# Retention and two FFNs: the loads of q and k parted by tokens from the fourth chunk on

## The chip, the cores and the metric

The program runs on one core of a Trainium2 chip. The metric is the device time of one execution in microseconds (us), as the median of several runs. TensorE is called PE here, VectorE DVE, ScalarE ACT, GpSimd POOL and SyncE SP; PE's loads of its weights are PEld.

## What is computed

A retention layer over two batches, eight heads, 768 tokens and 64 channels, in float32, then two feed-forward layers (FFNs) on its output, 1536 tokens by 512. The layers are cut here to what matters:

```python
for b in range(nb):                                   # blocks of tokens
    intra = einsum('bhic,bhjc->bhij', qb, kb) * Dmask # Dmask: powers of lam
    intra = einsum('bhij,bhjd->bhid', intra, vb)
    inter = einsum('bhid,bhde->bhie', qb * lam_pow, kv_state)
    out[:, :, sl] = intra + inter
    kv_state = lam_block * kv_state + einsum('bhsd,bhse->bhde', kb * rev_pow, vb)
x = out as (1536, 512)
x = mish(x @ moe_w_in) @ moe_w_out                    # 512 -> 2048 -> 512
x = elu(x @ moe2_w_in) @ moe2_w_out
```

## The kernel before

**Retention** (lines 126 to 385) works on twelve chunks of 128 tokens, all eight heads of one batch at a time; chunk n is batch n % 2, tokens 128 * (n // 2) onwards. For each chunk q, k and v are loaded from HBM to tiles `qn`, `kn` and `vn` of 128 partitions (one token each) by 8 heads by 64 channels (`load`, lines 143 to 156). One transfer moves 256 KB; a piece of contiguous memory in it is one token of one head, 64 float32 or 256 bytes. Only chunk 0 is loaded in halves, of four heads each, so that work can begin early.

The loop at line 357 runs over n. At its head SP issues the loads of k and q of chunk n + 3 and of v of chunk n + 1, and in some rounds a weight tile of the first FFN (`raw`, 512 KB, `LOAD` at line 536). Then PE does, in this order: the scores of chunk n (`sc`, line 275), the transposes of chunk n + 1 (`Tp`, line 231, first k's, then q's, each in two halves of 64 tokens), and the outputs of chunk n - 1 (`o`, line 305: first the terms of q and the state `sbd`, then those of `am` and `vn`) with its new state (`st`, line 314). ACT copies the transposed tiles out of PSUM, DVE multiplies by the decay and keeps the state, POOL scales k (`kd`, line 255).

Four buffers stand behind each of `qn`, `kn` and `vn`, so a load waits only for the readers of the chunk four before. The order on each engine is that of the program (`pin`). All loads are issued by SP, one after the other, so an issue that is held holds all behind it. SP has eight semaphores for the completion of its DMAs and takes them in turn (DMAHW0 to DMAHW7 in the rows of the order below): a DMA waits until the one eight before it has landed.

**The FFNs** (lines 388 to 571) work on 512 tokens by 512 columns, with every float32 operand as a high and a low part and three matmuls for each product (lines 412 and 454). DVE and ACT make the two parts of each weight tile from `raw` (`w_steps`, lines 86 to 120); a few of these steps stand already in the last rounds of retention (`STEPS`, line 537), and SP loads each next weight tile when a buffer comes free (line 115).

Of the kernel before, what the change touches and what calls it, by code (L numbers as in the profile page):

```python
# [18 lines left out]
def kernel(  # L19
# [12 lines left out]
    nc = tc.nc  # L32
    P = 128
# [92 lines left out]
    def retention(beside_load, beside_step, at_end):  # L126
# [12 lines left out]
        def pin(ins):  # L139
            tc.keep_in_program_order(ins)  # L140
            return ins

        def load(n, names, parts=1):
            if not 0 <= n < NC:
                return
            b, c = chunks[n]
            for nm in names:
                nat[n, nm] = io.tile([P, H, D], F32, tag=nm + "n", name=nm + "n")
            for y in range(parts):
                for nm in names:  # L150
                    src, t = {"k": k, "q": q, "v": v}[nm], nat[n, nm]
                    hs = slice(y * H // parts, (y + 1) * H // parts)
                    pin(nc.sync.dma_start(  # L153
                        out=t[:, hs],
                        in_=src[b, hs, c * P:(c + 1) * P, :].rearrange("h p d -> p h d"),
                    ))

        lam_b = cst.tile([P, H, 1], F32, name="lam_b")
        load(0, "kq", 2)
        nc.scalar.dma_start(out=lam_b.rearrange("p h o -> p (h o)"), in_=lam.partition_broadcast(P))  # L160
        load(1, "kq")
        load(2, "kq")
        load(0, "v")

# [7 lines left out]
        def powers(m, end):  # L172
# [19 lines left out]
            out=eye, in_=eye, compare_op=ALU.not_equal, fill=1.0, base=0,  # L192
# [7 lines left out]
            out=dm.rearrange("p h i -> p (h i)"),  # L200
# [357 lines left out]
    def first_units():  # L558
        for _ in todo:
            pass  # L560
        for u in range(EARLY):
            unit(u)
            weights_at(u)

    retention(beside_load, beside_step, first_units)
    open_late()
    for u in range(EARLY):
# [36 lines left out]
```

## Time and profile before

| | us |
|---|---|
| median of 3 runs (lowest to highest) | 583.84 (583.68 to 584.41) |
| the profiled execution, device time | 584.55 |
| its span, first to last instruction | 582.4 |
| PE busy in the span | 575.6 (99%) |
| retention, up to the first FFN matmul | about 54 |

The profile is of one execution, whose device time is 2.15 us above its span and 0.71 us above the median. It shows PE in the granted clock of 2.4 GHz (1.00 of full speed) in all slices. The views used are the page, the instructions of PE and SP in order of time with what ended the idle time before them, the DMA queues of a stretch, the DMA issues of a stretch with their time to landing, and the busy time of a stretch. A queue named "instruction" carries the engines' own instructions; q1 carries SP's loads.

### The profile page before, as it was taken

To read this page: it belongs to the slowest core of one execution; us is meant where nothing else is said; L and a number is where in the kernel's file an instruction comes from. 1 tells how busy PE (TensorE), PEld (TensorE's weight loads), DVE (VectorE), ACT (ScalarE), POOL (GpSimd) and SP (SyncE) were. 2 spreads that over 40 slices of the span, in tenths; PEclk is the share of its full clock that TensorE was granted. 3 is DMA by queue.
4 is the path that set the end of the run, shared out by engine and by line. 5 is a ranking of instruction groups with operands and counts; after the bars stand their busy time and mean duration, and the time that the engine had idled before them with its cause. 6 is when DMAs were issued, how large, how long until landed. Compare 5 with 4: busy or idle time off the path is not lost.

```text
span 582.4 us, 8137 instructions
## 1 busy us (share of the span) xinstructions
PE 575.6 (99%) x3240; PEld 481.9 (83%) x3240; DVE 431.1 (74%) x798; ACT 231.5 (40%) x390; POOL 18.8 (3%) x28
## 2 busy tenths in 40 slices
PE   8999999999999999999999999999999999999997
PEld 7888888888888888888888888888888888888886
DVE  5779999998399726993599956995499957944342
ACT  3655554344134124233346445555145235235220
POOL 5330000000000000000000000000000000000000
PEclk9999999999999999999999999999999999999999
DMA  9998333344023301322022221321022310000112
GB/s 189 194 221 233 109 109 109 109 114 140 1 73 109 108 2 36 108 77 70 0 73 72 74 72 37 109 77 69 2 72 73 108 37 0 2 0 1 72 55 91
DMA packets 61029, 46.66 MB, mean 80 GB/s; under 512 B 38848, under 2 KB 55488, under 8 KB 60992
## 3 DMA queue, kind: packets, MB, share of 16 engines
q1 hardware_dynamic: 60848, 46.14, 27.8%
q8 instruction: 25, 0.41, 0.3%
q14 instruction: 12, 0.10, 0.1%
q10 hardware_dynamic: 144, 0.00, 0.0%
HBM read 43.00 MB, written 3.15 MB: 79 GB/s over the span
## 4 chain that ended last, share of the span: by engine, by line
PE 93%; DMA 2%; DVE 2%; SPq 2%; issue 0%; ACT 0%; ACTq 0%
PE h L412 44%; PE y L454 43%; DMA vn<-in_v_dram 2%; PE o L305 2%; PE y L469 2%; SPq L153 2%; PE sc L275 1%; PE st L314 0%; PE Tp L231 0%; DVE b L104 0%; DVE u L111 0%; DVE xl L333 0%; DVE q L263 0%; DVE am L283 0%; ACT T L237 0%
## 5 line engine op out<-in xcount | busy, mean ns | idle before, releaser
L412 PE MATMUL h<-xh,w 128*128 128x512 f32 x768 | 240.8, 389 | 0.2 <-ACT w L118 0.2
L412 PEld LDWEIGHTS h<-xh,w 128*128 128x128 f32 x768 | 144.2, 188 | 30.5 <-ACT w L118 0.6
L412 PE MATMUL h<-xl,w 128*128 128x512 f32 x384 | 149.4, 389 | 0.0
L454 PE MATMUL y<-w,g 128*128 128x512 f32 (+1 forms) x588 | 132.5, 385 | 0.0
L454 PEld LDWEIGHTS y<-w,g 128*128 128x128 f32 x588 | 108.9, 188 | 22.0
L454 PE MATMUL y<-g,w 128*128 128x512 f32 x528 | 121.5, 389 | 0.0
L454 PEld LDWEIGHTS y<-g,w 128*128 128x128 f32 x528 | 99.1, 188 | 20.5
L482 DVE TENSOR_TENSOR acc<-acc,y 128x512 f32<-128x512 f32 (+1 forms) x73 | 49.5, 679 | 58.5 <-PE y L454 58.5
L422 DVE TENSOR_TENSOR g<-g,g 128x512 fp32r<-128x512 f32 x96 | 66.0, 689 | 30.0 <-ACT g L421 27.2
L412 PEld LDWEIGHTS h<-xl,w 128*128 128x128 f32 x384 | 72.1, 188 | 14.8
L118 ACT ACTIVATE w<-m 128x512 fp32r<-128x512 f32 x64 | 40.2, 628 | 102.1 <-PE h L412 55.2
L421 ACT ACTIVATE g<-g 128x512 fp32r<-128x512 f32 x96 | 60.2, 628 | 16.3 <-DVE g L439 14.8
L119 DVE TENSOR_TENSOR w<-m,w 128x512 fp32r<-128x512 f32 x64 | 44.1, 688 | 24.3 <-ACT w L118 23.7
L430 ACT ACTIVATE g<-h 128x512 f32<-128x512 f32 x48 | 28.5, 597 | 71.1 <-PE h L412 71.1
L436 ACT ACTIVATE e<-h 128x512 f32<-128x512 f32 x48 | 28.6, 596 | 59.0 <-PE h L412 58.0
L439 DVE SCALAR_TENSOR_TENSOR g<-e,h 128x512 f32<-128x512 f32 x48 | 32.9, 685 | 17.0 <-ACT e L437 17.0
L104 DVE SCALAR_TENSOR_TENSOR b<-raw,b 128x512 int32<-128x512 int32 x64 | 44.3, 693 | 0.4
L111 DVE SCALAR_TENSOR_TENSOR u<-raw,u 128x512 f32<-128x512 uint32 x64 | 43.9, 687 | 0.2
L116 DVE TENSOR_TENSOR m<-b,u 128x512 f32<-128x512 f32 x64 | 43.9, 687 | 0.1
L437 ACT ACTIVATE e<-e 128x512 f32<-128x512 f32 x48 | 30.2, 630 | 1.1
L98 DVE TENSOR_SCALAR m<-m 128x512 f32<-128x512 f32 x64 | 27.3, 428 | 0.1
L107 DVE TENSOR_SCALAR u<-b 128x512 int32<-128x512 int32 x64 | 27.0, 423 | 0.4
(50 smaller groups left out, 306.2 us busy)
## 6 DMA issues: line engine op xcount, KB each, us to landing
raw<-in_moe_w_in_dram SPq DMA_DIRECT2D x32, 512.0 KB, 3.8
raw<-in_moe_w_out_dram SPq DMA_DIRECT2D x32, 512.0 KB, 3.3
vn<-in_v_dram SPq DMA_DIRECT2D x12, 256.0 KB, 5.5
kn<-in_k_dram SPq DMA_DIRECT2D x11, 256.0 KB, 5.2
qn<-in_q_dram SPq DMA_DIRECT2D x11, 256.0 KB, 5.2
out_dram<-acc SPq DMA_DIRECT2D x11, 256.0 KB, 2.0
kn<-in_k_dram SPq DMA_DIRECT2D x2, 128.0 KB, 3.1
qn<-in_q_dram SPq DMA_DIRECT2D x2, 128.0 KB, 3.3
```

What stands on the lines that cost most here:

```text
L104: yield nc.vector.scalar_tensor_tensor(out=b, in0=hw, scalar=-0x40000000, in1=b, op0=ALU.bitwise_and, op1=ALU.bitwise_or)
L111: yield nc.vector.scalar_tensor_tensor(out=uf, in0=lw, scalar=2.0 ** -52, in1=uf, op0=ALU.mult, op1=ALU.mult)
L116: yield nc.vector.tensor_tensor(out=mf, in0=bf, in1=uf, op=ALU.add)
L118: nc.scalar.activation(out=w[:, 0], in_=mf, func=AF.Copy)
L119: yield nc.vector.tensor_tensor(out=w[:, 1], in0=mf, in1=w[:, 0].bitcast(F32), op=ALU.subtract)
L412: nc.tensor.matmul(h, lhsT=lt, rhs=rt, start=(kk == 0 and n == 0), stop=(kk == KD - 1 and n == 2),)
L421: nc.scalar.activation(out=gg[:, 0], in_=g, func=AF.Copy)
L422: nc.vector.tensor_tensor(out=gg[:, 1], in0=g, in1=gg[:, 0].bitcast(F32), op=ALU.subtract)
L437: nc.scalar.activation(out=e, in_=e, func=AF.Exp, scale=-1.0)
L439: nc.vector.scalar_tensor_tensor(out=g, in0=e, scalar=-1.0, in1=h, op0=ALU.add, op1=ALU.max)
L454: nc.tensor.matmul(y, lhsT=lt, rhs=rt, start=(i == 0 and n == 0), stop=(i == G - 1 and n == 2),)
L482: nc.vector.tensor_tensor(out=dst, in0=dst, in1=y, op=ALU.add)
```

## The change

From chunk 3 on, `load` issues q in two DMAs instead of one, of tokens 0 to 119 and 120 to 127, and k in two: by n % 4 they are 126 and 2, 108 and 20, 117 and 11, 110 and 18 tokens. The transfer of v, the first three chunks and all else stay. The bytes and the pieces of 256 bytes are the same, 1024 to a tile.

```diff
+        def rows_of(n, nm):
+
+            if n < 3 or nm == "v":
+                return ()
+            if nm == "q":
+                return (120,)
+            return ((126,), (108,), (117,), (110,))[n % 4]
...
-                    pin(nc.sync.dma_start(
-                        out=t[:, hs],
-                        in_=src[b, hs, c * P:(c + 1) * P, :].rearrange("h p d -> p h d"),
-                    ))
+                    ends = (0,) + rows_of(n, nm) + (P,)
+                    for r0, r1 in zip(ends, ends[1:]):
+                        pin(nc.sync.dma_start(
+                            out=t[r0:r1, hs],
+                            in_=src[b, hs, c * P + r0:c * P + r1, :].rearrange("h p d -> p h d"),
+                        ))
```

Lines after it move down by ten. On SP, v of chunk 0, then k and q of chunk 3 and v of chunk 1 stand like this before:

```order
L153 DMA vn<-in_v_dram 128x8x64 [waits DMAHW1_49]
L153 DMA kn<-in_k_dram 128x8x64 [waits DMAHW2_49]
L153 DMA qn<-in_q_dram 128x8x64 [waits DMAHW3_49]
L153 DMA vn<-in_v_dram 128x8x64 [waits DMAHW4_49]
```

And now, with SP's row of a round three DMAs long before and five long after:

```order
L163 DMA vn<-in_v_dram 128x8x64 [waits DMAHW1_49]
L163 DMA kn<-in_k_dram 110x8x64 [waits DMAHW2_49]
L163 DMA kn<-in_k_dram 18x8x64 [waits DMAHW3_49]
L163 DMA qn<-in_q_dram 120x8x64 [waits DMAHW4_49]
L163 DMA qn<-in_q_dram 8x8x64 [waits DMAHW5_49]
L163 DMA vn<-in_v_dram 128x8x64 [waits DMAHW6_49]
```

Each chunk from the fourth on has two more DMAs, 18 in all, and two more of the eight completion semaphores. On PE the transposes of chunk 3 and the outputs of chunk 1 stand like this before:

```order
L231 MATMUL Tp<-ident,kn 128x64 [waits DMAHW2_49,DVE_49]
L231 MATMUL Tp<-ident,kn 128x64 x7
L231 MATMUL Tp<-ident,qn 128x64 [waits DMAHW3_49]
L231 MATMUL Tp<-ident,qn 128x64 x7
L305 MATMUL o<-am,vn 64x128 [waits DMAHW4_49,DVE_49]
L305 MATMUL o<-am,vn 64x128 x7
```

And now:

```order
L241 MATMUL Tp<-ident,kn 128x64 [waits DMAHW2_49,DVE_49]
L241 MATMUL Tp<-ident,kn 128x64 [waits DMAHW3_49]
L241 MATMUL Tp<-ident,kn 128x64 x6
L241 MATMUL Tp<-ident,qn 128x64 [waits DMAHW4_49]
L241 MATMUL Tp<-ident,qn 128x64 [waits DMAHW5_49]
L241 MATMUL Tp<-ident,qn 128x64 x6
L315 MATMUL o<-am,vn 64x128 [waits DMAHW6_49,DVE_49]
L315 MATMUL o<-am,vn 64x128 x7
```

The second matmul of each group, which reads the upper 64 tokens, waits for the second DMA. No instruction of PE, DVE, ACT or POOL is added or moved; POOL's `kd` waits for both DMAs of its k.

## Rows read from the trace of the kernel before

**Rows 1.** The page: busy us (share of the span) and instructions of each engine

```profile
PE 575.6 (99%) x3240; PEld 481.9 (83%) x3240; DVE 431.1 (74%) x798; ACT 231.5 (40%) x390; POOL 18.8 (3%) x28
```

**Rows 2.** TensorE in order of time: start us, us, line, out<-in, idle before

```profile
14.51 0.47 PE L231 MATMUL Tp<-ident,kn 64*128 64x64 f32 x8
...
16.36 1.09 PE L305 MATMUL o<-am,vn 128*64 128x128 f32 x16 [0.56 <-DMA vn<-in_v_dram]
...
22.79 0.41 PE L231 MATMUL Tp<-ident,kn 64*128 64x64 f32 x8
...
23.38 1.09 PE L305 MATMUL o<-q,sbd 128*64 128x128 f32 x16
```

**Rows 3.** TensorE in order of time, later in the same loop

```profile
33.64 1.16 PE L275 MATMUL sc<-T 64*128 64x128 f32 x16
...
36.16 1.04 PE L305 MATMUL o<-am,vn 128*64 128x128 f32 x16
...
37.59 1.16 PE L275 MATMUL sc<-T 64*128 64x128 f32 x16
...
41.34 1.09 PE L305 MATMUL o<-am,vn 128*64 128x128 f32 x16
```

**Rows 4.** SyncE in order of time: start us, us that the issue held it

```profile
2.85 0.51 SPq L153 DMA_DIRECT2D kn<-in_k_dram  x1
...
6.54 1.10 SPq L153 DMA_DIRECT2D vn<-in_v_dram  x1
7.68 1.32 SPq L153 DMA_DIRECT2D kn<-in_k_dram  x1
9.04 1.14 SPq L153 DMA_DIRECT2D qn<-in_q_dram  x1
10.23 1.14 SPq L153 DMA_DIRECT2D vn<-in_v_dram  x1
...
12.66 2.30 SPq L153 DMA_DIRECT2D qn<-in_q_dram  x1
...
25.78 2.17 SPq L153 DMA_DIRECT2D vn<-in_v_dram  x1
...
30.36 0.91 SPq L153 DMA_DIRECT2D vn<-in_v_dram  x1
31.32 1.53 SPq L75 DMA_DIRECT2D raw<-in_moe_w_in_dram  x1
...
34.67 2.45 SPq L153 DMA_DIRECT2D vn<-in_v_dram  x1
```

**Rows 5.** DMA queues of 12.0:14.5: packets, MB, share of 16 engines

```profile
q8 instruction: 1, 0.02, 3.3%
```

**Rows 6.** DMA of 14.5:19.2 in 40 slices of 0.12 us

```profile
GB/s 233 231 172 163 133 113 100 41 37 46 115 174 133 129 235 270 283 270 235 218 185 129 61 78 148 176 218 279 283 281 268 255 264 231 238 248 264 231 248 251
```

**Rows 7.** DMA issues at 6.54, 7.68, 9.04, 10.23: count, KB, us to landing

```profile
vn<-in_v_dram SPq DMA_DIRECT2D x1, 256.0 KB, 5.2
kn<-in_k_dram SPq DMA_DIRECT2D x1, 256.0 KB, 5.2
qn<-in_q_dram SPq DMA_DIRECT2D x1, 256.0 KB, 6.2
vn<-in_v_dram SPq DMA_DIRECT2D x1, 256.0 KB, 6.0
```

**Rows 8.** The same for the issues at 30.36, 31.32, 34.67

```profile
vn<-in_v_dram SPq DMA_DIRECT2D x1, 256.0 KB, 4.9
raw<-in_moe_w_in_dram SPq DMA_DIRECT2D x1, 512.0 KB, 6.1
vn<-in_v_dram SPq DMA_DIRECT2D x1, 256.0 KB, 6.6
```

**Rows 9.** Line 81 on SyncE, later: issue ns min/median/max

```profile
L81 SPq DMA_DIRECT2D raw<-in_moe_w_out_dram x32: 327/336/341, 51.5 to 467.2; - x32
```

**Rows 10.** 54 to 62 us: busy us (instructions) by engine, clock, DMA share, GB/s

```profile
54.00:62.00 8.00, 7.84 (x59) 6.29 (x58) 7.87 (x18) 2.62 (x5) 0.00 (x0) 1.00 0.28 90
```

## The prediction

> **What bounds the kernel now.** I read the page first: PE is busy for 575.6 of the 582.4 us [rows 1]. Most of that lies in the FFNs, behind the change, and there PE runs without a gap. So a gain can only be idle time of PE in retention, and it is kept only if what follows moves up with it. I then read PE in order of time and looked for the places where one round of the loop takes longer than the next. There are two where a DMA ended the wait.
>
> The first is in the round of chunk 2. From the first transpose of k to the outputs behind the transposes it takes 16.36 - 14.51 = 1.85 us; an undisturbed round takes 23.38 - 22.79 = 0.59 us. PE loses **1.26 us**, first to q of chunk 3, then to v of chunk 1 [rows 2]. The second is in the round of chunk 8. From the scores to the outputs on `vn` an undisturbed round takes 36.16 - 33.64 = 2.52 us, this one 41.34 - 37.59 = 3.75. PE loses **1.23 us** [rows 3]. Together that is 2.49 us, and it is all that the loads cost PE in the rounds that the change reaches.
>
> Next I asked why those loads are late. The landings stand in the rows of the single issues: v of chunk 0 at 6.54 + 5.2 = 11.7, k of chunk 3 at 7.68 + 5.2 = 12.9, q of chunk 3 at 9.04 + 6.2 = 15.2, v of chunk 1 at 10.23 + 6.0 = 16.2 [rows 4, 7]. One step is 1.2 us, the next 2.4, the next 1.0. The step of 2.4 us goes with one 16 KB packet of the instruction queue, the only one in 12.0 to 14.5 [rows 5]. It took 3.3% of 16 engines in 2.5 us, so 1.3 us of one engine. SP's issue of that time is held for 2.30 us, against 1.1 to 1.3 before it [rows 4], and then the whole stream falls to 37 GB/s for a moment, from above 230 [rows 6]. I read this as one DMA engine being blocked by the instruction fetch, its queue filling, SP standing at that queue, and the other fifteen running dry. Another issue that is held for over 2 us stands at 25.78 [rows 4].
>
> The second stall has the same cause summed up. From 11.7 to v of chunk 7 at 34.67 + 6.6 = 41.3 there are 21 transfers of 256 KB and one weight tile. The tile takes 37.4 - 35.3 = 2.1 us (31.32 + 6.1 against 30.36 + 4.9) [rows 4, 8], so the 21 take 27.5 us, 1.31 each. A round has three, 3.93 us, which is what PE needs for a round (37.59 - 33.64 = 3.95 [rows 3]). The stream has nothing to spare, and the weight tile puts it behind.
>
> **What the change does, part by part.**
>
> *The bytes* are the same and cost nothing.
>
> *Fewer tokens for some engines.* A DMA of fewer than 128 tokens need not use all sixteen engines evenly. If the engine that fetches instructions is among those relieved, it takes the 1.3 us of a fetch without holding SP, and a transfer returns to its step of 1.2 us (11.7 to 12.9 [rows 4, 7]). No row here tells how the tokens are dealt out, nor which engine fetches. The Trainium skill does ("DMA: Bandwidth & Descriptors", the section on why a DMA increments its semaphore by 16): a DMA from SP uses the largest number of engines up to 16 that divides its tokens, and the lowest-numbered ones. By that q would leave the last engine idle and k the last two to five, while the busiest engine carries 27 to 29 tokens of a chunk's three tensors instead of 24; at the two rates of the next paragraph the sum for a chunk would be 3.4 to 4.3 us by it. No run here shows that yet.
>
> *More tokens for others.* What is taken from some engines goes to the rest. At a step of 1.2 us for 8 tokens an engine takes 0.15 us per token. An engine that is behind does better: the step after the fetch is 1.0 us [rows 4, 7], 0.125 us per token. So the parting has a price between nothing (the full engines run at the rate of one that catches up) and 0.15 us for each small part (they run at the common rate, and one has a token more).
>
> *Eighteen more DMAs on SP.* The shortest issue in the trace takes 0.34 us (median of 32 [rows 9]), and the same 256 KB whose issue now takes 1.1 us took 0.51 when nothing stood before it [rows 4]. So SP is held by full queues, not by its own work: three issues at 0.51 and two at 0.34 are 2.2 us of a round of 3.95. Each is also issued over four transfers ahead (5.2 us to landing against 1.2 a step). The cost per small part lies between 0 and 0.34 us, and I take **0.07 us** for both prices together, a fifth of that end, since the queue ahead covers most of it and the engine's faster rate most of the rest.
>
> *More waits.* PE waits twice more in a chunk, before the second matmul of each group; behind it stand the transposes, the outputs and the next scores. The second part is issued right behind the first, so this is the old wait with a later name, and its cost is in the 0.07. POOL's `kd` waits for two DMAs; PE needs it only a round later. SP waits for the DMA eight before, now 1.6 chunks back (6.3 us at 3.95) instead of 2.7; landings take 4.9 to 6.6 us [rows 7, 8]. It may hold SP now and then, but seven DMAs, over four of them large, still stand in the queues, so I count nothing. If that cover is gone, it is the issue's 0.34 again.
>
> *The sum.* First stall: k, q and v after 11.7 land in three steps of 1.2, plus two small parts, 0.14: v of chunk 1 at 15.4. PE would reach it at 16.36 - 1.26 = 15.1, so with the 0.15 us that it started after the landing before, a stall of 0.45 remains and 0.8 us is gained (0 to 1.26). Second stall: 21 steps of 1.2, the tile's 2.1 and 14 small parts (seven chunks) of 0.07, 1.0: 25.2 + 2.1 + 1.0 = 28.3, so v of chunk 7 lands at 40.0 instead of 41.3. The first gain is part of this one. PE is **1.3 us** ahead at this point, and after it only two parted chunks follow. Ends: with the small parts at 0, v lands at 39.0, and PE is ahead by 2.3; with both stalls gone it is 2.49, the most that can be had. With 0.34 each, 14 cost 4.8, v lands at 43.8, and PE is 2.5 us behind.
>
> *Does the rest move up?* From 54 to 62 us DVE is busy for 7.87 of 8.00 and PE for 7.84 [rows 10]; DVE's chain there hangs on PE's last rounds, so both shift together. The weight tiles are in the same stream and move up too. I count no loss. The profiled execution would go from 584.55 to 583.2, the median from 583.84 to **582.5 us**.
>
> **The rivals.**
>
> *No difference: the price eats the relief.* With 0.15 us a small part, 14 cost 2.1, v of chunk 7 lands at 41.1, and 0.2 us is left: 583.6. For it speaks the step of 1.2 us that holds whenever all engines work; against it the 1.0 us after the fetch.
>
> *Slower: the fetching engine is not relieved.* If that engine is one of those that get more, each fetch still holds SP, and its own queue is longer. Then nothing of 2.49 is gained and the price comes on top: 18 parts of 0.15, 2.7 us, less what a round can hide. I take 2.4: 586.2. It decides as soon as the engine has a token more than before, and the rows say nothing against it but that the change takes its tokens always from the same end.
>
> *Slower: SP becomes the bound.* If each added issue costs its 0.34 us in the stream, PE is 2.5 us behind at v of chunk 7, and the last four parts add 1.4, of which a round can hide some 0.7: 3.2 us, 587.0. This begins where five issues no longer fit between two rounds; 2.2 of 3.95 us speak against it. A rule of the Trainium skill speaks for it: the same page ("Rules for kernel authors") says that transfers under 64 KB are mostly overhead and that a transfer parted by partitions gains nothing, because the parts share the engines. The small parts here are 4 to 40 KB; no row shows one of that size. By that rule the time is this rival's.
>
> *The relief is there and goes lost later*, in the DVE-bound stretch: the time would be that of no difference, and it is counted there.
>
> **How the numbers follow.** A measurement of this kernel can tell about 0.2%, 1.17 us, from no change. The forecast, faster by over 0.2%, has 0.47: 582.5, its own range 581.3 to 582.6. No difference has 0.28; its values reach from 582.7 to 585.0. An unrelieved engine has 0.18 and SP as the bound 0.07, both slower by over 0.2%. The range from 581.3 (both stalls gone) to 586.2 (the engine not relieved, taken whole) leaves out the SP rival and some of the tails, under 2 in 10. Faster 0.47, same 0.28, slower 0.25.
>
> **What would show it.** Right: no SP issue of over 2 us beside a packet of the instruction queue in the rounds of chunks 2 to 6; no dip of the stream near 15.4 us; q of chunk 3 landing before 14.8 and v of chunk 1 near 15.4; v of chunk 7 near 40; the first FFN matmul 1 to 2 us earlier, and the same number of us off the end. Wrong: steps of 1.3 us or more between landings of whole chunks' tensors without a fetch beside them, issues of the small parts near 0.5 us with nothing before them, or PE waiting for the second part of a k or q. If the landings move up and the end doesn't, the last step, that the rest follows, is what failed.

## The result, and the profile after

The change makes the kernel slower: 588.77 us (588.18 to 589.47, 4 runs) against 583.86 us (583.68 to 584.41), a ratio of 1.0074 with an interval of 1.0059 to 1.0089. That is 4.9 us where 1.3 us less were forecast. The profiled execution after took 588.18 us with a span of 586.0, against 584.55 and 582.4 before.

The page after: the busy time of PE, the packets of SP's queue, and the chain that ended last.

```profile
PE 578.6 (99%) x3240; PEld 484.2 (83%) x3240; DVE 430.7 (73%) x798; ACT 231.4 (39%) x390; POOL 19.1 (3%) x28
...
q1 hardware_dynamic: 60951, 46.15, 28.4%
...
PE h L422 44%; PE y L464 43%; DMA qn<-in_q_dram 4%; PE y L479 2%; SPq L163 2%; PE warm L225 1%; PE o L315 1%; PE sc L285 1%; PE Tp L241 1%; ACT T L247 0%; DVE u L111 0%; POOL kd L265 0%; DVE b L104 0%; DVE u L107 0%; PE st L324 0%
```

PE has the same 3240 matmuls as in [rows 1]. New in the chain is `qn<-in_q_dram`. The four longest pieces of that chain up to 60 us (start us, us, what) show where these loads sit.

```profile
23.81 4.59 DMA qn<-in_q_dram
...
31.43 5.29 DMA qn<-in_q_dram
...
36.94 5.92 DMA qn<-in_q_dram
...
46.89 4.91 DMA qn<-in_q_dram
```

Between 23 and 52 us the end of the kernel hangs on q's transfers for 20.7 us, and between them on PE and on SP's issues. PE in order of time (columns as in [rows 2]) shows the round that stalled before, and the one of chunk 8:

```profile
16.65 0.46 PE L241 MATMUL Tp<-ident,kn 64*128 64x64 f32 x8 [0.19 <-DVE q L273]
...
17.29 1.09 PE L315 MATMUL o<-am,vn 128*64 128x128 f32 x16
...
39.52 1.16 PE L285 MATMUL sc<-T 64*128 64x128 f32 x16
41.07 0.68 PE L241 MATMUL Tp<-ident,kn 64*128 64x64 f32 x8 [0.39 <-DMA kn<-in_k_dram]
42.90 0.46 PE L241 MATMUL Tp<-ident,qn 64*128 64x64 f32 x8 [1.15 <-DMA qn<-in_q_dram]
43.30 1.09 PE L315 MATMUL o<-q,sbd 128*64 128x128 f32 x16
44.22 1.04 PE L315 MATMUL o<-am,vn 128*64 128x128 f32 x16
```

From the first transpose of k to the outputs, the round of chunk 2 now takes 17.29 - 16.65 = 0.64 us instead of 1.85 [rows 2]: in this profile the first stall is gone (the runs on the start of PE show why). But PE is at 17.29 where it was at 16.36. In the round of chunk 8 the scores are 44.22 - 39.52 = 4.70 us ahead of the outputs, where 3.75 us lay before and 2.52 in an undisturbed round [rows 3]; PE now stands for k (0.39 us) and then for q (1.15). SP in order of time (the two parts of a tensor are one row):

```profile
12.24 1.96 SPq L163 DMA_DIRECT2D kn<-in_k_dram  x2
14.30 1.30 SPq L163 DMA_DIRECT2D qn<-in_q_dram  x2
15.64 0.95 SPq L163 DMA_DIRECT2D vn<-in_v_dram  x1
16.70 2.45 SPq L163 DMA_DIRECT2D kn<-in_k_dram  x2
19.25 0.82 SPq L163 DMA_DIRECT2D qn<-in_q_dram  x2
20.11 0.87 SPq L163 DMA_DIRECT2D vn<-in_v_dram  x1
21.09 2.62 SPq L163 DMA_DIRECT2D kn<-in_k_dram  x2
```

A round of SP takes 16.70 - 12.24 = 4.46 and 21.09 - 16.70 = 4.39 us, more than the 3.95 that PE needs [rows 3]. What that means for the loads is in one row of a view by stretches: 12 to 44 us, the busy time of each engine, the clock, the DMA share, GB/s. Before:

```profile
12.00:44.00 32.00, 30.43 (x598) 28.50 (x597) 23.95 (x38) 18.53 (x30) 11.55 (x14) 1.00 1.01 209
```

After:

```profile
12.00:44.00 32.00, 29.72 (x572) 27.68 (x574) 21.91 (x33) 16.86 (x28) 11.16 (x13) 1.00 1.01 192
```

**The loads move 192 GB/s instead of 209.** The same bytes take 8.9% longer; over the 46 us from 8 to 54 us that would be 4.1 us. The first FFN matmul starts at 57.79 instead of 54.05, 3.7 us later, and the profiled executions differ by 588.18 - 584.55 = 3.6 us.

That reading holds for every kernel that was run. In this table, ordered by time, the last column is the profiled execution's time less the start of the first FFN matmul:

| kernel | profiled run, us | GB/s, 12 to 44 us | first FFN matmul, us | rest, us |
|---|---|---|---|---|
| 18 extra loads of 2 tokens | 583.54 | 217 | 53.18 | 530.4 |
| q, k by heads, 4 and 4 | 583.62 | 213 | 53.28 | 530.3 |
| before | 584.55 | 209 | 54.05 | 530.5 |
| q, k, v by heads | 584.58 | 209 | 54.07 | 530.5 |
| before, late start | 584.82 | 208 | 54.29 | 530.5 |
| only k parted | 585.62 | 202 | 55.22 | 530.4 |
| even and odd tokens | 585.88 | 205 | 55.56 | 530.3 |
| by heads, 7 and 1 | 586.21 | 199 | 55.83 | 530.4 |
| only q parted | 586.51 | 199 | 56.08 | 530.4 |
| 112, 8 and 8 tokens | 588.17 | 193 | 57.89 | 530.3 |
| after | 588.18 | 192 | 57.79 | 530.4 |
| 64 and 64 tokens | 588.45 | 191 | 58.11 | 530.3 |
| after, early start | 588.95 | 191 | 58.58 | 530.4 |
| v issued by ACT | 589.29 | 217 | 58.71 | 530.6 |

The rest is 530.3 to 530.6 us in all of them: whatever retention loses or gains arrives at the end unchanged. And but for the last row the time goes with the load rate, with 3 GB/s or so of scatter. (These are single runs, up to 0.9 us from the median of their kernel, and 1.8 with 112, 8 and 8 tokens.) So the question is what lowers the rate.

### The profile page after: what moved, and what is told of

The parts are those of the page before. It is cut to its first block, busy times and chain, and to the rows that moved or that the text cites. A ratio compares the mean times of both kernels' runs of the same rounds, so it can differ in the third digit from the quotient of the medians.

```text
span 586.0 us, 8162 instructions
## 1 busy us (share of the span) xinstructions
PE 578.6 (99%) x3240; PEld 484.2 (83%) x3240; DVE 430.7 (73%) x798; ACT 231.4 (39%) x390; POOL 19.1 (3%) x28
## 3 DMA queue, kind: packets, MB, share of 16 engines
q1 hardware_dynamic: 60951, 46.15, 28.4%
## 4 chain that ended last, share of the span: by engine, by line
PE 92%; DMA 4%; SPq 2%; DVE 1%; ACT 1%; issue 0%; POOL 0%; POOLq 0%; ACTq 0%
PE h L422 44%; PE y L464 43%; DMA qn<-in_q_dram 4%; PE y L479 2%; SPq L163 2%; PE warm L225 1%; PE o L315 1%; PE sc L285 1%; PE Tp L241 1%; ACT T L247 0%; DVE u L111 0%; POOL kd L265 0%; DVE b L104 0%; DVE u L107 0%; PE st L324 0%
```

## The experiments

The times are medians; the kernel before, run beside them, had 584.41, 584.43, 584.38, 584.42 and 583.98 us in the five comparisons.

### One part of the change alone

Only q parted, into 120 and 8:

```diff
-            if n < 3 or nm == "v":
+            if n < 3 or nm != "q":
```

> Only q is parted, into 120 and 8 tokens; k stays whole. Nine DMAs more instead of 18. The change took 4.9 us; three theories of it. (A) The engines that carry the instruction fetch are not relieved and get more of k: the trace of the changed kernel shows two landings late in DMAs of 11 and more engines, one late in those of 10, none in those of 9 or 8, so these engines would be the tenth and eleventh. Parted as 120 and 8, q leaves both with 8 tokens as before, so about 0: 583.3 to 584.5. (B) The busiest engines set the pace: they get 9 tokens of q instead of 8, 9 of the 35 tokens that the change adds in nine chunks, so a quarter of 4.9: 585.1. (C) Every added DMA costs the same: half of it, 586.3. (D) The late rise of PE's pace at the start of the profiled run (10.5 instead of 5.8 us) is half of the loss and has nothing to do with how tokens are parted: it shows again, with 2 us or so.

Only k, in its four cuts:

> Only k is parted as in the change; q stays whole. (A) All of the added tokens on the two late engines come from k (18 and 14 of them in nine chunks), so all of the loss: 588 to 589. (B) 26 of 35 tokens: 587.5. (C) Half: 586.3.

q alone took 587.12 us (ratio 1.0046, 1.0034 to 1.0059), k alone 585.62 (1.0022, 1.0013 to 1.0031). Both lose, 2.7 and 1.2 us, and the sum, 3.9, is near the 4.9 of the whole. It isn't k's uneven cuts, which load engines most unequally, that cost most.

### Other cuts by tokens

All engines even, 64 and 64 tokens for q and k; and 112 tokens on all engines with two parts of 8, which gives the low eight engines the most:

```diff
-            return ((126,), (108,), (117,), (110,))[n % 4]
+            return (64,)          # the other run: return (112, 120)
```

> k and q from chunk 3 on in two DMAs of 64 tokens each: as many DMAs as in the change (18 more than before), every engine with the tokens that it had. (A) and (B): no loss, 583.3 to 584.5. (C) All of the loss, 588 to 589. PE's waits are as in the change.

> k and q from chunk 3 on in three DMAs, of 112, 8 and 8 tokens: 36 DMAs more than before. By the count of completions 112 tokens go to sixteen engines, 7 each, and 8 tokens to the lowest eight, so the upper eight carry 22 tokens of a chunk instead of 24, and the lower eight 26. (A) The late engines are relieved, and the held issues go: 581.4 to 583. (B) 18 tokens more on the busiest engines against 35 in the change: 586.3. (C) Twice the loss: 593 to 594.

The halves took 588.35 us (1.0080, 1.0062 to 1.0098), as slow as the change, with no engine given more than another. Three parts took 586.35 (1.0037, 1.0023 to 1.0050; the profiled run in the table, 588.17, was the longest of the five), with twice as many added transfers as the change and less of a loss. Here alone SP also waits before loads of q, k and v for earlier ones to land, 3.9 us in all between 6 and 52 us: a round has seven loads on the eight semaphores. So neither an uneven share nor the count of transfers alone explains it.

### The start of PE

In the profile after, PE's first matmuls keep a slow pace until 10.5 us, before until 6.0 (the granted clock reads 1.00 in both), and the first outputs start at 13.80 us instead of 11.84. One warm-up matmul more in the kernel after, and three fewer in the kernel before, turn this round:

```diff
-        warm(7)
+        warm(8)               # after; the other run: before with warm(4)
```

> The changed kernel with eight instead of seven matmuls on idle data ahead of the first transposes, so that PE does not stand idle before the first data. (D) If the late rise of PE's pace is part of the loss, the rise comes near 6 us again and the time falls by up to 2 us, to 586.5. If the loads set the end of retention anyway, the rise comes early and the time stays at 588 to 589.

> The kernel before the change with four instead of seven such matmuls, so that PE stands idle longer before the first data and its pace rises late, as in the profile of the changed kernel. (D) 2 us slower than before, 586. If the loads set the end of retention, under 0.6 us.

The first outputs of the kernel after, with the early pace:

```profile
11.84 1.09 PE L315 MATMUL o<-am,vn 128*64 128x128 f32 x16 [0.28 <-DMA vn<-in_v_dram]
```

and of the kernel before with the late one:

```profile
13.44 1.09 PE L305 MATMUL o<-am,vn 128*64 128x128 f32 x16
```

The first still takes 588.75 us (1.0077, 1.0061 to 1.0092), the second 584.50 (1.0004, 0.9995 to 1.0013). PE can be 1.6 us late at its first outputs and the first FFN matmul comes only 0.24 us later, since the loads set the pace behind it. The late start is not the cause.

But it is what took the first stall away. The round of chunk 2 in the kernel after with the early start:

```profile
14.34 0.46 PE L241 MATMUL Tp<-ident,kn 64*128 64x64 f32 x8
...
16.06 1.09 PE L315 MATMUL o<-am,vn 128*64 128x128 f32 x16 [0.70 <-DMA vn<-in_v_dram]
```

and in the kernel before with the late one:

```profile
16.27 0.47 PE L231 MATMUL Tp<-ident,kn 64*128 64x64 f32 x8 [0.19 <-DVE q L263]
...
16.92 1.10 PE L305 MATMUL o<-am,vn 128*64 128x128 f32 x16
```

Parted and early, the round takes 1.72 us, nearly the 1.85 of before, and PE still waits for v; whole and late, it takes 0.65. PE no longer stands there because it comes later than the load, not because the load comes much earlier.

### The count of issues

The kernel before, with a load of 2 tokens into a spare tile behind each load of q and k from the fourth chunk on:

> The kernel before the change, with its tiles whole, and behind each k and q from chunk 3 on a DMA of two more tokens (4 KB) to a tile that nothing reads: as many added DMAs as the change has, 18, no transfer parted, no engine but the lowest two with more to carry, and nothing on the two late engines. (A) No loss, 583.3 to 584.8. (C) All of it, 588 to 589. (E) A fixed cost on the engines used only, which are not the late ones: under 1.2 us, 583.8 to 585.

584.00 us (0.9992, 0.9984 to 1.0001). Eighteen more transfers and issues, 4 KB each, cost nothing that can be measured.

### The loads alone

One kernel issued nothing but loads, in six series of twelve tiles:

> All computation is left out and the output is zeros: SP issues six series of twelve tiles of 256 KB without a pause, so that the price of a part is measured by itself, with no instruction fetch of PE beside it. The series: whole tiles; halves of 64 tokens; whole again; 120 and 8; 126 and 2, 108 and 20, 117 and 11, 110 and 18 in turn; 112, 8 and 8. From the kernel with halves I read about 0.68 us from part to part against 1.2 for a whole tile. (E) Every DMA costs the engines that it uses a fixed time besides its bytes, some 0.16 us: a tile takes 1.2 us whole, 1.36 in halves, about 1.4 in the mixed parts. (B) The busiest engine sets the pace at 0.15 us a token: 1.2 whole, 1.2 in halves, 1.35 as 120 and 8, 1.5 to 1.8 in the mixed parts, 1.35 as 112, 8 and 8. (C) SP's issue sets it: two to three issues at 0.3 to 0.4 us are under 1.2, so 1.2 in all series.

By stretches inside the six series, in their order (no PE there; the last two columns are the DMA share and GB/s):

```profile
4.00:12.00 8.00, 0.00 (x0) 0.00 (x0) 1.00 1.33 220
16.00:28.00 12.00, 0.00 (x0) 0.00 (x0) 1.00 1.27 200
36.00:42.00 6.00, 0.00 (x0) 0.00 (x0) 1.00 1.35 218
48.00:58.00 10.00, 0.00 (x0) 0.00 (x0) 1.00 1.14 201
65.00:77.00 12.00, 0.00 (x0) 0.00 (x0) 1.00 0.81 181
80.00:92.00 12.00, 0.00 (x0) 0.00 (x0) 1.00 0.86 194
```

Whole tiles move 218 to 220 GB/s, 1.20 us for 262,144 bytes. Parted by tokens they move less, in every form: halves 200 (1.31 us), 120 and 8 201 (1.30), k's four cuts 181 (1.45), 112 and 8 and 8 194 (1.35). No engine computes here. **Parting by tokens has a price of its own in the stream**, 0.10 to 0.25 us a tile (one series of twelve tiles each).

I then thought that the queue holds transfers by number, so that parted ones leave fewer bytes in it and a fetch empties it sooner. Two runs were to show this, one of the stream beside a busy PE, one of the kernel parted by heads:

> The six series of loads of the run without computation again (whole tiles, halves of 64 tokens, whole tiles, 120 and 8, the four cuts of k in turn, 112 and 8 and 8; no retention, no FFN, zeros written), and beside them TensorE now runs 2100 small matmuls in a row, so that its instructions have to be fetched as in the kernel. Without them the series moved 218, 200, 218, 201, 181 and 194 GB/s (1.20, 1.31, 1.20, 1.30, 1.45 and 1.35 us a tile of 256 KB). Theory F (the queue of loads holds a number of transfers, so parted loads leave fewer bytes in it, and a fetch that holds one engine for 1.3 us costs a parted stream more): whole tiles stay at 1.20 to 1.25 us, the parted series rise by 0.1 us a tile or more above their own values. Rival G (the fetch costs the same whatever is loaded, and the parted stream is simply slower by its own price): every series rises by the same few hundredths.

Its small matmuls took 421 ns each, so only four instruction packets came in the 100 us of loads; on fetches it decided nothing. It shows how well the series repeat: in the same stretches 218, 185, 219, 189, 189 and 204 GB/s. Whole tiles come out as before; the parted forms move by 8 to 15 GB/s, two down and two up, and stay below the whole ones. So the price of a parted form is uncertain by up to 0.1 us a tile.

> The kernel before with q and k from the fourth chunk on in two transfers each as in the run of halves, but parted by heads: 128 tokens of four heads, twice, so every transfer has all tokens. If what costs is that there are 18 more transfers of smaller size in the queue (theory F, or a price for each transfer on all engines), the time is that of the halves by tokens: 587.5 to 588.5. If it is tokens that matter (which engine gets how many, or partitions below 128), this form is free: 584.

```diff
+                    two = (hs,)
+                    if n >= 3 and nm != "v":
+                        two = slice(0, H // 2), slice(H // 2, H)
+                    for hs in two:
                         pin(nc.sync.dma_start(out=t[:, hs], ...))
```

583.61 us (0.9988, 0.9974 to 1.0002). This is the run that decides. Its transfers have the number, the size and the order of the halves, 128 KB each, but all 128 tokens of four heads. From 12 to 44 us, by heads:

```profile
12.00:44.00 32.00, 31.00 (x614) 29.10 (x613) 24.48 (x39) 18.54 (x31) 11.58 (x14) 1.00 0.99 213
```

and in halves of 64 tokens:

```profile
12.00:44.00 32.00, 29.09 (x544) 26.65 (x544) 21.49 (x33) 16.96 (x27) 11.07 (x13) 1.00 0.99 191
```

213 against 191 GB/s, and 4.7 us between the medians. My theory of the queue fell with it: what costs in the halves is that a transfer has fewer than 128 tokens.

### Which property of the tokens

In the kernel, even and odd tokens:

> The kernel before with q and k from the fourth chunk on in two transfers each, even tokens and odd tokens: 64 partitions each as in the halves (588.35), but every second one, so that each transfer spreads over all of the 128 partitions. Theory P (it matters which partitions a transfer covers: one that covers a block of them is written by all engines into that block at once): near the run by heads, 583.6 to 585. Theory R (it matters that the rows that an engine reads lie together in DRAM, 8 in a row before, 4 in the halves, none here): 588 or more. Theory N (any transfer of fewer than 128 partitions is slow, wherever they lie): 588.

```diff
-        two = slice(0, H // 2), slice(H // 2, H)             # heads
+        two = slice(0, P, 2), slice(1, P, 2)                 # tokens
```

586.38 us (1.0037, 1.0019 to 1.0055), between the theories: not free, and not as slow as the halves. The bare stream with the same theories:

> Loads alone again (no retention, no FFN, zeros written), six series of 12 tiles of 256 KB: two transfers by heads, halves of 64 tokens, even and odd tokens, four transfers of 32 tokens, whole tiles whose tokens lie two rows apart in DRAM, whole tiles. Whole tiles took 1.20 us and halves 1.31 (200 GB/s) in the stream before. Theory P: by heads 1.20, halves 1.31, even and odd 1.20, quarters 1.35 or more, rows apart 1.20. Theory R: by heads 1.20, halves 1.31, even and odd and rows apart 1.35 or more. Theory N: by heads and rows apart 1.20, halves and even and odd 1.31, quarters more.

The six series in their order:

```profile
4.00:13.00 9.00, 0.00 (x0) 0.00 (x0) 1.00 1.08 223
17.00:29.00 12.00, 0.00 (x0) 0.00 (x0) 1.00 1.00 198
34.00:46.00 12.00, 0.00 (x0) 0.00 (x0) 1.00 0.85 193
50.00:70.00 20.00, 0.00 (x0) 0.00 (x0) 1.00 0.57 129
74.00:84.00 10.00, 0.00 (x0) 0.00 (x0) 1.00 1.28 221
88.00:98.00 10.00, 0.00 (x0) 0.00 (x0) 1.00 1.31 220
```

By heads 223, halves 198, even and odd tokens 193, quarters of 32 tokens 129, whole tiles whose tokens lie two rows apart in HBM 221, whole tiles 220. Rows that don't lie together in HBM cost nothing (221). Spreading 64 tokens over every second partition doesn't help (193). Of the three theories only N, the number of partitions in the transfer, fits this stream. In the kernel it isn't the whole account: even and odd tokens lost 2.0 us there, the halves 3.9. The quarters have a second limit: 48 issues took SP 24.41 us, 0.51 each, and four of them are 2.0 us a tile.

The Trainium skill says the same of the number ("SBUF — State Buffer", the section "Door 1: The DMA port swizzle (why `[64,N]` ≈ `[32,N]`)"): use all 128 partitions, since 64 in one block reach 8 of the 16 ports. The 198 GB/s of the halves lie near its 196 for 64 partitions, but it gives 328 for 128 partitions (both for transfers of 1 MiB), where the whole tiles of 256 KB here move 220. Its reason doesn't show here: even and odd tokens would reach all sixteen ports by its table, and were no faster.

And back in the kernel, unequal parts with all tokens in both:

> The kernel before with q and k from the fourth chunk on in two transfers each, seven heads and one head, all 128 tokens in both: the same 18 added transfers as in the change and the small ones of 32 KB, near its 4 to 40 KB, but every transfer covers all partitions and every engine has the same share. If small transfers cost as such, it is slower, 586 to 588. If the cost lies in parting the tokens alone, 583.5 to 584.5, as by heads in halves.

585.89 us (1.0023, 1.0009 to 1.0037). With all 128 tokens in both parts it still loses 1.5 us: for q and k equal parts by heads are free, unequal ones are not. That a small part costs as such is not what the extra loads of 4 KB showed; this difference is open. The change parts unequally too, so how much of its 4.9 us is due to this and how much to the tokens is not shown.

### Fetches beside the stream, and two other forms

> Loads alone (no retention, no FFN, zeros written), six series of 12 tiles of 256 KB: whole tiles, two transfers by heads, halves of 64 tokens, even and odd tokens, 120 and 8, the four cuts of k in turn; beside them TensorE runs 2400 transposes of the kernel's form in a row, two instructions each, so that instructions are fetched as often as in the kernel (a 16 KB packet about every 6 us). Without fetches these forms moved 219, 223, 199, 193, 201 and 181 GB/s. Theory F2 (after a fetch the late engine has to catch up, and in a parted transfer it catches up more slowly, so each fetch costs a parted stream more): whole tiles and heads lose up to 5%, to 208 or more; the halves, even and odd, 120 and 8 and the cuts lose 8% or more, to 183, 178, 185 and 166 or less. Rival G (a fetch costs the same whatever is loaded): all six lose the same share.

Here PE fetched until 84 us, a packet in about 4.4 us where the kernel before has one in 6.4 (five in 12 to 44 us), so the last series ran without fetches. The first four series as a whole, and the part of the fifth in which PE fetched:

```profile
2.00:17.00 15.00, 14.77 (x413) 14.50 (x411) 0.00 (x0) 0.00 (x0) 1.00 1.05 202
18.00:35.00 17.00, 15.84 (x490) 15.43 (x488) 0.00 (x0) 0.00 (x0) 1.00 0.80 179
36.00:54.00 18.00, 17.78 (x550) 17.38 (x546) 0.00 (x0) 0.00 (x0) 1.00 0.75 168
55.00:73.00 18.00, 17.12 (x522) 16.57 (x518) 0.00 (x0) 0.00 (x0) 1.00 0.73 163
76.00:84.00 8.00, 7.35 (x229) 7.14 (x226) 0.00 (x0) 0.00 (x0) 1.00 0.84 180
```

Whole tiles fall from 220 to 202 GB/s, halves by heads from 223 to 179, halves by tokens from 198 to 168, even and odd from 193 to 163, 120 and 8 from 201 to 180: 8, 20, 15, 16 and 10%. But these stretches hold 2, 4, 4, 4 and 2 instruction packets. For each packet the stream loses 0.6, 0.8, 0.7, 0.7 and 0.4 us. So fetches cost every form, and no more where it is parted by tokens than whole or by heads; to this accuracy the prices add up. By heads, which is free in the kernel, loses most here; why is open.

> The kernel before, nothing parted, but the loads of v from chunk 1 on are issued by ScalarE instead of SyncE, so that there are two queues and SyncE's holds only k and q. If it is the one queue standing still at a fetch that costs the kernel before its two stalls (2.5 us), a second queue keeps the engines fed: 582 us or a little less. If the stalls come from the bytes as such (25 tiles at 1.2 us and what the fetches take), nothing changes: 584. If ScalarE pays for the issues (about 0.5 us of its time a chunk, beside 2.5 of 4 that it is busy), slower: 585 or more.

589.59 us (1.0090, 1.0063 to 1.0118). The loads moved 217 GB/s, more than before (and as much as in the kernel with extra loads, where SP issues all), and the kernel was still the slowest of all. The waits of PE up to 60 us (waiter, what it waited for: us in total, times, longest) show why:

```profile
PE sc L276 <- ACT T L238: 3.4, 3, 2.1
PE o L306 <- DVE xl L334: 1.5, 4, 0.6
```

ACT's copies of the transposes come late, and PE waits for them, up to 2.1 us at a time. ACT in order of time around one of its loads:

```profile
19.19 0.60 ACT L326 ACTIVATE xh<-o 128x512 fp32r<-128x512 f32 x1
22.48 0.37 ACTq L154 DMA_DIRECT2D vn<-in_v_dram  x1
22.95 1.02 ACT L238 ACTIVATE T<-Tp 128x1024 f32<-128x1024 f32 x1 [3.16 <-PE o L306]
```

The last row puts its wait down to PE, but the load between stands longer: its issue takes 0.37 us, but ACT stands before it from 19.79 to 22.48 us. By the completions in the trace, the earlier load of k whose semaphore this load takes lands at 22.46: the turn of eight semaphores, which now goes over both engines, holds ACT.

> The kernel before with q, k and v from the second chunk on in two transfers each by heads, all 128 tokens in both: 33 added transfers of 128 KB. By heads is free in the stream (223 GB/s against 220), and the halves of q and k alone gave 583.6. If the finer steps help PE at the two places where it waits, 583 or a little less; if nothing is to be had there, 584; if the number of transfers costs after all (eight semaphores, SyncE's issues of 0.5 us), 585 or more.

585.44 us (1.0024, 1.0007 to 1.0041). Finer steps give PE nothing, and the median is 1.5 us longer than before, with an interval above 1: what the expectation had for the case that the number of transfers costs after all. The profiled run, 584.58, was one of the three shortest of ten and shows no loss, so where it arises is open. Of the forms that were tried, none is faster than the kernel before by more than the measurement can tell.

## Why the prediction was wrong

**Two stalls of 2.49 us, due to loads: right for before.** That the first stall is gone in the profile after is luck: it goes with the late start, not with the parting. With the early start PE reached the outputs behind it at 16.06 us, 0.3 us sooner than before, where 0.8 were forecast.

**A fetch blocks one engine, and the stream runs dry: right in kind.** In the stream of loads alone, whole tiles fell from 220 to 202 GB/s when PE fetched.

**The parting relieves the engine that fetches: wrong, and the first step that failed.** In 12.5 to 21 us the two instruction packets took 1.6% of sixteen engines, 1.1 us each, much as the 1.3 us before [rows 5]. By the completions in the trace, from the first packet to 36 us, in the transfers on eleven engines or more one or two of the engines come in 0.5 to 1.7 us behind the others, in the one on ten engines one, in those on nine or fewer none. So the late ones would be the tenth and eleventh, which the change leaves at 24 tokens of a chunk (q's cut) or gives more (k's). The sign that the prediction set for this step misled. SP's issues for k between 12 and 31 us, one by one (shortest, median and longest in ns):

```profile
L163 SPq DMA_DIRECT2D kn<-in_k_dram x10: 639/1147/1422, 12.2 to 30.7; - x10
```

No issue is held for over 2 us (q's and v's are under 1), which was to speak for relief; but there are two for each k now, and the pair is held for 1.93 to 2.62 us in every one of these rounds, with a packet beside it or without. The rival "the fetching engine is not relieved" named this; it stopped at 586.2 us because it priced the rest too low.

How tokens are dealt out is shown by the packets of SP's queue, 60,951 after (the page in the section on the result), 103 more than before:

```profile
q1 hardware_dynamic: 60848, 46.14, 27.8%
```

The Trainium skill's rule in "DMA: Bandwidth & Descriptors" (why a DMA increments its semaphore by 16) agrees to the packet: with one closing packet for each engine, q's cuts use 15 + 8 engines nine times and k's 20, 16, 22 or 24, together 391, against 18 x 16 = 288 before. 391 - 288 = 103; q alone should have 63 more, k alone 40 and the halves 288, and they have 60,911, 60,888 and 61,136.

**The price of a small part, 0.07 us with an end at 0.34: mis-sized, and asked for in the wrong unit.** I priced the small part: its tokens, its issue. In the bare stream the whole tile gets slower, q's by 0.10 us and k's by 0.25. A chunk goes from 3.60 to 1.20 + 1.30 + 1.45 = 3.95 us, which is just what PE needs [rows 3], so the fetches and the weight tile would have nothing left to be absorbed in. Nine chunks give 9 x 0.35 = 3.2 us of the 3.7 by which the first FFN matmul is later; that the sum comes so near is partly luck, since its two parts don't fit singly (below). My term for eighteen parts was 18 x 0.07 = 1.3. I had looked for what an added DMA costs and not asked whether the large part, with 108 to 126 tokens instead of 128, still loads at the old rate: no row of before had a transfer of fewer than 128 tokens in a full stream, and I took its rate as given.

**SP as the bound: wrong as a mechanism, near as a time.** The rival gave 587.0. But eighteen more issues cost nothing in the run with extra loads, and the halves by heads have the same issues and are free. The rule of the Trainium skill that it leaned on ("DMA: Bandwidth & Descriptors", "Rules for kernel authors"), that transfers under 64 KB are mostly overhead, did not show with 4 KB each, behind a full queue. Some price of added transfers isn't excluded: the parts of seven heads and one, the smaller of 32 KB, and all three tensors by heads lost 1.5 us each.

**v of chunk 1 at 15.4, v of chunk 7 at 40:** the first outputs show it best: PE reached those of chunk 7 at 44.22 us, not 1.3 us before 41.34 [rows 3] but 2.9 behind. **The rest shifts along: right**, to 0.3 us in fourteen kernels.

**What stays open.** The bare prices don't give the kernel's losses one by one, though they are uncertain by up to 0.1 us a tile, 0.9 us in nine. Halves cost 2 x 0.11 us a chunk in the stream, 2.0 in nine, and 4.1 us in the kernel's profile; k's cuts alone 2.2 by price and 1.2 measured; q's cut 0.9 and 2.0 (2.7 between the medians). That fetches make a stream parted by tokens dearer is not borne out by the run beside a fetching PE. Why a transfer of fewer than 128 partitions is slower, with every engine at the same share, no run here shows: neither the spread of the partitions nor the neighbourhood of the rows in HBM is it.

## What to carry to other kernels

When a stream of loads paces a kernel, look at its rate in GB/s over the stretch before and after a change: here it orders nearly all kernels by time, where stalls of single rounds moved about and misled. If a load has to be parted, part it along the free dimension in equal pieces and leave all 128 partitions in each transfer (free here for q and k, not for all three tensors); before parting for a finer balance, measure the new shape alone in a stream of loads. And price what a change does to the large remainder, not only the small piece that it cuts off.

## What the runs showed of the hardware that I had not expected

- A load of 64 of 128 partitions moves 198 to 200 GB/s where one of the same size with all 128 moves 223; even when every second partition is taken, 193.
- Tokens that lie two rows of 256 bytes apart in HBM load as fast as adjacent ones, 221 GB/s against 220.
- Beside a PE that fetches its instructions, a stream of whole tiles falls by 8%, from 220 to 202 GB/s, with two packets in 15 us.
- Loads of v issued by ACT cost 5.2 us at a load rate of 217 GB/s: each issue takes 0.37 us, but ACT stands before it until an earlier load has landed.
- PE can start its outputs 1.6 us late without the kernel's time changing (584.50 against 584.43).
